# Moving the inverse DFT tables, splitting the last stage into pairs, and letting the first pairs skip a relayout: a fused attention and spectral-mixing kernel

## The chip, the cores and the metric

The kernel runs on one core of a Trainium2 chip. The metric is the device time of one execution in microseconds, as the median of several executions. All inputs start in the chip's main memory (HBM) and the output ends there. In the texts below PE is the matrix engine, DVE the vector engine, ACT the scalar engine, POOL the engine that here issues the weight, q and k transfers (with a cast to bf16 on the way), and SP the engine that issues the other transfers. PSUM is the memory of eight banks into which PE writes.

## The reference, cut to what matters

```python
def phi(x):                                    # q, k, v: 8 batches, 8 heads, 576 rows, 64 wide
    proj = einsum('bhsd,df->bhsf', x, w_phi)   # 64 -> 128 features
    proj = proj - max(abs(proj), axis=-1, keepdims=True)
    return concatenate([exp(proj), exp(-proj)], axis=-1)
num = phi(q) @ (phi(k)^T v);  den = phi(q) @ sum(phi(k)) + 1e-6
x = (num / den) reshaped to (8, 576, 512)      # heads side by side

X = rfft(x, axis=1)                            # along the 576 rows
Yr = Xr @ w_r[m] - Xi @ w_i[m]                 # for each of the first 64 modes m,
Yi = Xr @ w_i[m] + Xi @ w_r[m]                 # with a 512 x 512 matrix of its own
y = irfft(Y (other modes 0), n=576, axis=1)
u = x + y
out = u + maximum(u @ w_ch, 0)                 # w_ch: 512 x 512
```

The weights `w_r` and `w_i` are 64 x 512 x 512 in f32 each, 134 MB together. Everything else that is read is about 29 MB, and 9.4 MB are written.

## The kernel before, in words

**Order.** Two kinds of wrapper keep every instruction of an engine in the order in which the program text gives it (`InOrder`), so the text below is also the order of each engine's queue. That holds for the queues of POOL and SP too: an issue that has to wait for a free buffer holds up all issues behind it.

**Attention.** The work is cut into 16 units (`Unit`): four groups of two heads (g) times four pairs of batches (bp). A loop over n from -1 to 16 (lines 480 to 548) works on several units at once: P = unit n - 1 gets its forward Fourier transform (`freq`), Q = unit n its attention sums and quotients (`num`), K = unit n + 1 its features, R = unit n + 2 the turning of k. In the same stage the loads of later units are issued (`load_q`, `load_k`, `load_v`). q, k and v have two buffers each. `xs` holds the quotients of all units as bf16.

**Mixing.** A weight transfer (`wload`) brings eight modes of one of the two weights, for one group of 128 input channels, as 1 MB of bf16. There are 64 of them, each used by one `mix` of eight matmuls. They wait in the eight slots of pool `pw`, and the first ones also in five other places (`home`: memory of `yacc`, `XT` and `xs` that isn't needed yet). `next_w` issues the next transfer. `some(x)` does x mixes from the list `mixq` and, unless the mix used one of the five places, issues one transfer after each. A group's mixes come free when its fourth unit has had its `freq`, so the first mixes run in stage n = 4. X in the loop says how many mixes a stage does.

**Tables.** `CF` is the forward table. It is made from a table of sines `csf` at the start (`forward_table`, stage -1). The inverse tables `CI` and `CL` are made from the same `csf` in stage n = 0 (`inverse_table`): each of five blocks is scaled on DVE, transposed on PE in f32 and copied back by DVE.

**After the attention** (lines 549 to 672) 22 mixes are left. Between them items of a list `todo` are done (`fill`): first 37 items that turn each of the 36 chunks of x (128 rows by 512) and multiply it with `w_ch` into `xw` (`Channels`), then 36 calls of `absorb`, each of which adds the inverse transform of the first six octets of modes (48 modes) to one chunk of x and of xw. How many items go after a mix is n in that loop. The last eight mixes belong to octets 6 and 7. When an octet is complete, its sum `yst` and the product `zst` of that with `w_ch` are written by DMA into another layout (`put`): octets 0 to 5 into `yall` and `zall`, octets 6 and 7 into `yl`, two copies each, one copy issued by SP and one by ACT.

**The last stage** (lines 675 to 698) makes the 36 output chunks, in pairs and for each pair of batches one single chunk. For each chunk PE puts x and xw into two banks through the identity, adds the last two octets from `yl` with `CL`, ACT takes the ReLU of one (`rl`) and DVE adds the other (`of`). Four chunks fill an `of` tile of 1 MB, which SP stores; the single chunk (`ofr`) is stored as two pieces of 128 KB.

Of the kernel before, what the change touches and what calls it, by code (L numbers as in the profile page):

```python
# [10 lines left out]
F32 = mybir.dt.float32  # L11
BF16 = mybir.dt.bfloat16
# [8 lines left out]
NG = 4  # L21
# [22 lines left out]
def kernel(  # L44
# [260 lines left out]
    ident_f = const.tile([128, 128], F32, name="ident_f")  # L305
    make_identity(nc, ident_f)
    ident_b = const.tile([128, 128], BF16, name="ident_b")
    dve.tensor_copy(ident_b, ident_f)
# [3 lines left out]
    sp.dma_start(wpf[64:128, :], w_phi)  # L312
    si = const.tile([128, 5], I32, name="si")
# [5 lines left out]

    units = [Unit(g, bp) for g in range(NG) for bp in range(NP)]  # L320
    units[0].load_k()
    units[0].load_v()
    units[0].load_q()
# [9 lines left out]

    clear(XTb[0])
    wchb = const.tile([128, 4, 512], BF16, name="wchb")
    CF = const.tile([128, 6, 4, 64], BF16, name="CF")
    CI = const.tile([128, 5, 128], BF16, name="CI")
    CL = const.tile([128, 5, 128], BF16, name="CL")
# [35 lines left out]
    def inverse_table():  # L374

        cio = scr[:, 640:1280].rearrange("p (c m t r) -> p c m t r", c=5, t=2, r=2)
        for r in range(2):
            for t in range(2):
                dve.tensor_scalar_mul(
                    out=cio[:, :, :, t, r], in0=csf[:, :, r, 32 * t:32 * t + 32],  # L380
                    scalar1=(2.0 - 4.0 * r) / S_)
        for c in range(5):
            dve.tensor_scalar_mul(
                out=cio[:, c, 0, 0, :], in0=cio[:, c, 0, 0, :], scalar1=0.5)
            pct = one([128, 128])
            flat = cio[:, c].rearrange("p m t r -> p (m t r)")
            pe.transpose(pct, flat, ident_f)
            dve.tensor_copy(CI[:, c, :], pct)
            late = scr[:, 128 * c:128 * c + 128]
            dve.tensor_copy(  # L390
                late.rearrange("p (s m) -> p s m", s=4),
                flat[:, 96:128].unsqueeze(1).to_broadcast([128, 4, 32]))
            pct = one([128, 128])
            pe.transpose(pct, late, ident_f)
            dve.tensor_copy(CL[:, c, :], pct)


    def home(g, w):

        if g == 0 and w < 2:  # L400
            t = yacc.bitcast(BF16).rearrange("p o e -> p (o e)")[:, 4096 * w:4096 * w + 4096]
        elif g == 0 and w == 2:
            t = XTb[1].rearrange("p s b m -> p (s b m)")[:, 0:4096]
        elif g == 0 and w in (10, 11):
            t = xs[:, w - 8].rearrange("p b n d -> p (b n d)")[:, 0:4096]
        else:
            return pw.tile([128, MG, DMODEL], BF16, name="wt", tag="wt")
        return t.rearrange("p (m e) -> p m e", m=MG)

    def wload(g, w):  # L410
        wt = home(g, w)
        o, i = w // 2, w % 2
        pool.dma_start(
            wt, (moe_w_r, moe_w_i)[i][MG * o:MG * o + MG, g * 128:(g + 1) * 128, :].rearrange(
                "m p e -> p m e"))
        return wt

# [30 lines left out]
    wts = {}  # L448
    wq = [(g, mg) for g in range(2) for mg in range(2 * NO)]
    wq += [(g, mg) for g in (2, 3) for mg in range(12)]  # L450
    wq += [(g, 2 * o + i) for o in (6, 7) for g in (2, 3) for i in range(2)]
    order = list(wq)
    mixq = []

    def next_w(n):
        for _ in range(n):
            if wq:
                key = wq.pop(0)
                wts[key] = wload(*key)

# [15 lines left out]
    next_w(1)  # L476
    units[0].cast_k()
    units[0].turn_k()
    units[2].load_k()
    for n in range(-1, len(units) + 1):  # L480
# [16 lines left out]
        if P:  # L497
            P.freq()
            if P.bp == NP - 1:
                mixq += [key for key in order if key[0] == P.g and (P.g < 2 or key[1] < 12)]  # L500
        if K:
            K.cast_q()
# [39 lines left out]
        if n == 0:  # L542
            inverse_table()
# [10 lines left out]
    pst = ctx.enter_context(tc.tile_pool(name="pst", bufs=8, space=bass.MemoryType.PSUM))  # L554
# [7 lines left out]
    zall = pb.tile([96, B_, DMODEL], BF16, name="zall", bufs=1)  # L562
    yall = pw.tile([128, B_, DMODEL], BF16, name="yall", tag="wt")
    yl = pw.tile([128, B_, DMODEL], BF16, name="yl", tag="wt")


# [20 lines left out]
    def back(p, c, bp, table, src, r):  # L587

        if c < 8:
            pe.matmul(p, lhsT=table[r, c % 4, :], rhs=src[r, 2 * bp + c // 4, :],  # L590
                      start=(src is yall), stop=True)
        else:
            for i in range(2):
                pe.matmul(p[64 * i:64 * i + 64, :], lhsT=table[r, 4, 0:64],
                          rhs=src[r, 2 * bp + i, :], start=(src is yall), stop=True)

    def absorb(bp, n):

        r = slice(0, 96)
        x = chunk(bp, n)  # L600
        p = bank()
        back(p, n, bp, CI, yall, r)
        dve.tensor_tensor(out=x, in0=p.rearrange("p (g e) -> p g e", g=4), in1=x, op=ALU.add)
        q = bank()
        pe.matmul(q, lhsT=ident_b, rhs=xw[:, bp, n, :], start=True, stop=False)
        back(q, n, bp, CI, zall, r)
        act.copy(xw[:, bp, n, :], q)
# [14 lines left out]
    todo += [lambda c=c: absorb(*c) for c in chunks]  # L622
# [6 lines left out]
    def put(src, o, dst, copies):  # L629
        if o < 6:  # L630
            sp.dma_start(dst[16 * o:16 * o + 16], src)
        else:
            for e, s in zip((sp, act), copies):
                r = 32 * s + 16 * (o - 6)
                e.dma_start(yl[r:r + 16], src)

    steps = len(mixq)
    while mixq:
        key = mixq.pop(0)
        g, o, i = key[0], key[1] // 2, key[1] % 2  # L640
        if key not in wts:
            next_w(1)
        mix(*key, wts.pop(key), XTb[g % 2], bank)
        next_w(1)
        left = len(mixq)
        n = 5 if left < 8 else max(1, -(-(len(todo) - 36 - 3) // (left - 7)))
        if left == 0:
            n = len(todo)
        if g == NG - 1 and i == 1:
            py = pys.pop(o)  # L650
            yst = pb.tile([128, DMODEL], BF16, name="yst")
            dve.tensor_tensor(out=yst, in0=py, in1=yacc[:, o, :], op=ALU.add)
            put(yst, o, yall, (0, 2))
            fill(min(n, 1))
            pt = bank([128, 4, 128], BF16)
            for dc in range(4):
                pe.transpose(pt[:, dc, :], yst[:, dc * 128:(dc + 1) * 128], ident_b)
            yT = pb.tile([128, 4, 128], BF16, name="yT")
            act.copy(yT, pt)
            fill(min(n - 1, 1))  # L660
            pz = bank()
            for dc in range(4):
                pe.matmul(
                    pz, lhsT=yT[:, dc, :], rhs=wchb[:, dc, :],
                    start=(dc == 0), stop=(dc == 3))
            zst = pb.tile([128, DMODEL], BF16, name="zst")
            act.copy(zst, pz)
            put(zst, o, zall, (1, 3))
            fill(max(n - 2, 0))
        else:  # L670
            fill(n)
    assert not todo


    for bp in range(NP):
        of = [pw.tile([128, 4, DMODEL], F32, name="of", tag="wt") for _ in range(2)]
        ofr = pb.tile([128, DMODEL], F32, name="ofr")
        for ns in ((0, 1), (2, 3), (4, 5), (6, 7), (8,)):
            pq = [(bank(), bank()) for _ in ns]
            for n, (p, q) in zip(ns, pq):  # L680
                pe.matmul(p.rearrange("p (g e) -> p g e", g=4), lhsT=ident_b,
                          rhs=chunk(bp, n), start=True, stop=False)
                pe.matmul(q, lhsT=ident_b, rhs=xw[:, bp, n, :], start=True, stop=False)
            for a, (n, (p, q)) in enumerate(zip(ns, pq)):
                for b, t in enumerate((p, q)):
                    r = 64 * a + 32 * b
                    back(t, n, bp, CL, yl, slice(r, r + 32))
            for n, (p, q) in zip(ns, pq):
                rl = pb.tile([128, DMODEL], F32, name="rl")
                act.activation(rl, q, ACT.Relu)  # L690
                o = of[n // 4][:, n % 4, :] if n < 8 else ofr
                dve.tensor_tensor(out=o, in0=p, in1=rl, op=ALU.add)
            if ns[-1] in (3, 7):
                i = ns[-1] // 4
                sp.dma_start(
                    out[2 * bp + i, 0:512, :].rearrange("(p c) e -> p c e", c=4), of[i])
        for i in range(2):
            sp.dma_start(out[2 * bp + i, 512:576, :], ofr[64 * i:64 * i + 64, :])
# [31 lines left out]
```

## Time and profile before

| | us |
|---|---|
| median of 8 runs (lowest, highest) | 481.69 (480.99, 482.95) |
| the profiled execution | 481.51 |
| its span, first to last instruction | 479.7 |
| busy in the span: PE, DVE, ACT, POOL | 337.5, 312.3, 277.1, 103.9 |

The span leaves out 1.8 us of the profiled execution's own time. The mean clock granted to PE was 0.87 of full speed. A busy time is a sum over stages that have different limits, so it doesn't say what a change in one stage is worth.

How the profile is read: its page gives, over 40 equal slices of the span, the busy share of each engine in tenths, the share of the 16 DMA engines and the GB/s that they wrote. The table by stage gives the same for chosen stretches; there the DMA share counts overlapping packets and stands at about 1.25 when the transfers never pause. The chain of waits follows the work that ended last back from the end: start, length and what it was. The waits view sums for each engine what it waited for: total, number of waits, longest. All instructions have the line of a helper (L37), so they are told apart by the tiles that they write and read, `out<-in`.

### The profile page before, as it was taken

How to read it: one execution, taken by the hardware profiler on the slowest of the kernel's cores; microseconds unless marked ns; L12 is line 12 of the kernel's file. 1: busy time of each engine (PE TensorE's matmuls, PEld its weight loads, DVE VectorE, ACT ScalarE, POOL GpSimd, SP SyncE). 2: the span in 40 equal slices, each digit the busy share in tenths (PEclk: the TensorE clock that was granted, in tenths of full speed). 3: DMA queues.
4: the chain of work that ended last, by engine and by line, in shares of the span. 5: the costliest groups of instructions: out<-in, count | busy, mean ns of one | idle time of the engine just before them, and what ended most of it. 6: DMA issues, size and time to landing. Idle time of an engine off the chain costs nothing.

```text
span 479.7 us, 8392 instructions
## 1 busy us (share of the span) xinstructions
PE 337.5 (70%) x3227; PEld 204.2 (43%) x3254; DVE 312.3 (65%) x568; ACT 277.1 (58%) x471; POOL 103.9 (22%) x139
## 2 busy tenths in 40 slices
PE   2552777876677787776857738559976577888894
PEld 1341455654555454554645426434433233333221
DVE  5677397796797788788787776752322113765695
ACT  3761477668679678658648628512433224565684
POOL 8332032112152142123032122041111111000000
PEclk9985567688998888889779777887999989999999
DMA  8999999998999999999999999999999999995398
GB/s 136 212 213 209 214 201 216 210 205 131 206 209 217 217 200 217 215 203 217 218 201 215 218 206 207 207 207 207 207 213 214 214 212 216 207 223 101 131 368 312
DMA packets 111896, 100.23 MB, mean 209 GB/s; under 512 B 17008, under 2 KB 110320, under 8 KB 110832
## 3 DMA queue, kind: packets, MB, share of 16 engines
q0 software_dynamic: 84496, 76.03, 97.6%
q1 hardware_dynamic: 26784, 23.14, 18.6%
q10 hardware_dynamic: 576, 0.52, 0.5%
q8 instruction: 25, 0.41, 0.3%
q14 instruction: 15, 0.12, 0.1%
HBM read 163.64 MB, written 9.44 MB: 361 GB/s over the span
## 4 chain that ended last, share of the span: by engine, by line
DMA 63%; DVE 10%; PE 9%; issue 9%; ACT 4%; POOL 2%; SPq 1%; DVEq 0%; POOLq 0%; ACTq 0%
DMA wt<-in_moe_w_i_dram 28%; DMA wt<-in_moe_w_r_dram 20%; DMA qb<-in_q_dram 8%; DMA kb<-in_k_dram 5%; PE pt L37 5%; PE one L37 4%; DVE mk L37 2%; POOL wt L37 2%; DVE va L37 2%; DVE nd L37 2%; DMA kf<-in_k_dram 2%; SPq L37 1%; DVE mq L37 1%; PE two L37 1%; ACT AB L37 1%
## 5 line engine op out<-in xcount | busy, mean ns | idle before, releaser
L37 ACT ACTIVATE AB<-two 128x1024 bf16<-128x1024 f32 x64 | 62.0, 1021 | 44.4 <-DVE mk L37 44.1
L37 ACT CAST xw<-pt 128x512 bf16<-128x512 f32 x72 | 41.9, 586 | 71.5 <-PE pt L37 66.4
L37 ACT ACTIVATE AQ<-two 128x1024 bf16<-128x1024 f32 x64 | 62.7, 1043 | 23.6 <-PE two L37 16.6
L37 DVE TENSOR_TENSOR nd<-one,e 128x390 f32<-128x390 f32 x48 | 26.9, 560 | 48.8 <-PE one L37 48.8
L37 POOL DMA_DIRECT2D wt<-in_moe_w_r_dram x29 | 25.6, 882 | 100.8 <-PE pt L37 35.1
L37 PE MATMUL one<-kvz,AQ 128*128 128x65 bf16 x512 | 30.1, 204 | 19.7 <-ACT kvz L37 14.5
L37 PE MATMUL one<-va,AB 128*128 128x65 bf16 x512 | 30.0, 219 | 18.9 <-DVE va L37 18.8
L37 DVE TENSOR_TENSOR va<-vn,ee 128x1152 bf16<-128x1152 f32 x32 | 42.0, 1357 | 0.0
L37 DVE COPY xT<-pt 128x512 bf16<-128x512 bf16 x36 | 15.2, 423 | 41.1 <-PE pt L37 41.1
L37 DVE TENSOR_REDUCE mk<-two 128x8 f32<-128x1024 f32 x32 | 39.0, 1220 | 4.0 <-PE two L37 4.0
L37 POOL DMA_DIRECT2D wt<-in_moe_w_i_dram x30 | 26.5, 882 | 67.6 <-PE pt L37 33.2
L37 PE MATMUL pt<-wchb,xT 128*128 128x512 bf16 x136 | 39.6, 410 | 0.8 <-DVE xT L37 0.5
L37 PEld LDWEIGHTS <-XT 128*32 128x32 bf16 x512 | 21.6, 165 | 42.6 <-issue 35.2
L37 PEld LDWEIGHTS <-xs 128*128 128x128 bf16 x304 | 29.2, 112 | 22.6 <-issue 11.8
L37 DVE TENSOR_REDUCE mq<-two 128x8 f32<-128x1024 f32 x32 | 37.7, 1217 | 1.1 <-PE two L37 1.1
L37 PEld LDWEIGHTS <-AQ 128*128 128x128 bf16 x512 | 25.3, 104 | 30.5 <-issue 27.3
L37 POOL DMA_DIRECT2D qb<-in_q_dram x32 | 22.9, 720 | 60.2 <-DVE nd L37 33.0
L37 PEld LDWEIGHTS <-AB 128*128 128x128 bf16 x512 | 25.3, 115 | 24.8 <-issue 12.9
L37 POOL DMA_DIRECT2D kb<-in_k_dram x32 | 22.9, 717 | 58.3 <-PE one L37 19.7
L37 DVE TENSOR_TENSOR xs<-pt,xs 128x512 bf16<-128x512 f32 x36 | 24.2, 691 | 13.5 <-PE pt L37 13.0
L37 PE MATMUL pt<-wt,XT 128*32 128x512 bf16 x176 | 15.6, 427 | 24.4 <-DMA wt<-in_moe_w_i_dram 14.6
L37 PE MATMUL one<-ident_b,kb 128*128 128x128 bf16 x144 | 15.8, 260 | 23.2 <-DMA kb<-in_k_dram 20.7
(94 smaller groups left out, 667.1 us busy)
## 6 DMA issues: line engine op xcount, KB each, us to landing
wt<-in_moe_w_i_dram POOLq DMA_DIRECT2D x30, 1024.0 KB, 27.0
wt<-in_moe_w_r_dram POOLq DMA_DIRECT2D x29, 1024.0 KB, 25.9
vn<-in_v_dram SPq DMA_DIRECT2D x32, 256.0 KB, 7.8
out_dram<-of SPq DMA_DIRECT2D x8, 1024.0 KB, 4.3
kb<-in_k_dram POOLq DMA_DIRECT2D x32, 128.0 KB, 20.5
qb<-in_q_dram POOLq DMA_DIRECT2D x32, 128.0 KB, 17.1
kf<-in_k_dram SPq DMA_DIRECT2D x32, 32.0 KB, 6.2
vn<-in_v_dram SPq DMA_DIRECT2D x32, 32.0 KB, 6.5
```

Source lines behind the costliest of these rows:

```text
L37: ins = f(*args, **kwargs)
```

## The change

- `inverse_table` is gone, and with it its f32 transposes. After the attention, `inverse_tables` computes `CI`, `CL` and a third table `CM` straight from integers, rows being modes: three iotas on POOL, bit fields of the row number and small scalars on DVE, then for each table a product, a reduction to one period, a sine on ACT and a scaling. It is the first item of `todo`.
- At the start the loads of unit 0's k and the first weight transfer go ahead of the identity and the iotas on POOL; q goes ahead of v; unit 0's k is turned before the forward table is computed.
- In stage n = 4 two mixes more are done, right after `freq`. One `next_w(1)` ahead of the loop moves to the start.
- `absorb` becomes a class `Absorb` of three steps; its last three chunks are spread over the end of the last mix. The number of items after each mix is counted anew.
- Both copies into `yl` are issued by SP.
- The last stage becomes a class `Last`: PSUM is split into two pools (four single banks for q, two double banks for p); the q side and ReLU of a pair are done one pair ahead of its p side; DVE adds two chunks in one instruction; each pair is stored by itself (512 KB).
- The first two pairs read only octet 6 from `yl` and take octet 7 straight from `yst` and `zst` with `CM`.

```diff
+    units[0].load_k()
+    next_w(1)
+    ident_f = scr[:, 2176:2304]
+    make_identity(nc, ident_f)
...
+    units[0].load_q()
+    units[0].load_v()
     si = const.tile([128, 5], I32, name="si")
     pool.iota(si[:, 0:4], [[1, 4]], base=0, channel_multiplier=4)
...
-    units[0].load_k()
-    units[0].load_v()
-    units[0].load_q()
...
+    units[0].cast_k()
+    units[0].turn_k()
     clear(XTb[0])
...
-    next_w(1)
-    units[0].cast_k()
-    units[0].turn_k()
     units[2].load_k()
...
                 mixq += [key for key in order if key[0] == P.g and (P.g < 2 or key[1] < 12)]
+            if n == 4:
+                some(2)
...
-        if n == 0:
-            inverse_table()
...
+    def inverse_tables():
+        flat = zall.rearrange("p b e -> p (b e)").bitcast(F32)
+        tok, ang, rnd = (flat[:, 640 * i:640 * i + 640] for i in range(3))
...
+        pool.iota(toki[:, 0:512], [[1, 4], [4, 128]], base=0, channel_multiplier=0)
+        pool.iota(toki[:, 512:640], [[0, 2], [1, 64]], base=512, channel_multiplier=0)
+        pool.iota(pi, [[0, 1]], base=0, channel_multiplier=1)
+        dve.tensor_copy(tok, toki)
...
+        def bits(src, shift, mask):
...
+            dve.tensor_scalar(out=t, in0=src, scalar1=shift, scalar2=mask,
+                              op0=ALU.logical_shift_right, op1=ALU.bitwise_and)
+            dve.tensor_copy(f, t)
...
+        for dst, m, r, only in ((CI, mode, r, None), (CL, late, r, None), (CM, last, rm, b0)):
+            n = 512 if only is not None else 640
...
+            dve.tensor_scalar(out=ang[:, :n], in0=tok[:, :n], scalar1=m, scalar2=ph,
+                              op0=ALU.mult, op1=ALU.add)
+            dve.tensor_scalar(out=rnd[:, :n], in0=ang[:, :n], scalar1=1.0 / S_, scalar2=MAGIC,
+                              op0=ALU.mult, op1=ALU.add)
+            dve.tensor_scalar(out=rnd[:, :n], in0=rnd[:, :n], scalar1=-MAGIC,
+                              scalar2=-float(S_), op0=ALU.add, op1=ALU.mult)
+            dve.tensor_tensor(out=ang[:, :n], in0=ang[:, :n], in1=rnd[:, :n], op=ALU.add)
+            act.activation(rnd[:, :n], ang[:, :n], ACT.Sin, scale=2.0 * math.pi / S_)
+            dve.tensor_scalar_mul(out=dst.rearrange("p c s -> p (c s)"), in0=rnd[:, :n],
+                                  scalar1=amp)
...
-            for e, s in zip((sp, act), copies):
+            for s in copies:
                 r = 32 * s + 16 * (o - 6)
-                e.dma_start(yl[r:r + 16], src)
+                sp.dma_start(yl[r:r + 16], src)
...
+    todo = [inverse_tables] + todo
...
-        n = 5 if left < 8 else max(1, -(-(len(todo) - 36 - 3) // (left - 7)))
-        if left == 0:
-            n = len(todo)
+        n = -(-max(len(todo) - 33, 0) // (left - 7)) if left > 7 else -(-len(todo) // max(left, 1))
...
+            if end:
+                ab[-3].sums()
+                ab[-3].keep_x()
...
             act.copy(yT, pt)
+            if end:
+                ab[-2].sums()
+                ab[-2].keep_x()
+                ab[-3].keep_w()
...
             put(zst, o, zall, (1, 3))
+            if end:
+                ab[-2].keep_w()
+                ab[-1].all()
...
+        def straight(self, which):
+            if self.early:
+                for a, n in enumerate(self.ns):
+                    pe.matmul((self.q if which else self.p)[a], lhsT=CM[:, n],
+                              rhs=(yst, zst)[which], start=False, stop=True)
...
+    seq = [Last(bp, ns) for bp in range(NP) for ns in ((0, 1), (2, 3), (4, 5), (6, 7), (8,))]
+    seq[0].base(1)
+    seq[0].late(1)
+    seq[0].straight(1)
+    seq[0].relu()
+    for g, s in enumerate(seq):
+        t = seq[g + 1] if g + 1 < len(seq) else None
+        if t:
+            t.base(1)
+        s.base(0)
+        if t:
+            t.late(1)
+        s.late(0)
+        s.straight(0)
+        if t:
+            t.straight(1)
+            t.relu()
+        s.store()
```

`base` puts x (0) or xw (1) of a pair into its banks, `late` adds the part from `yl`, `relu` is two ACT instructions into one tile, and `store` is the DVE add over both chunks and the issue of the store.

## The prediction

> **What bounds the kernel now.** I read the page first: its slices by time, then its bytes.
>
> ```profile
> DMA  8999999998999999999999999999999999995398
> GB/s 136 212 213 209 214 201 216 210 205 131 206 209 217 217 200 217 215 203 217 218 201 215 218 206 207 207 207 207 207 213 214 214 212 216 207 223 101 131 368 312
> ...
> HBM read 163.64 MB, written 9.44 MB: 361 GB/s over the span
> ```
>
> The span is 479.7 us and a slice 12. The DMA digit is 9 nearly everywhere up to slice 35, while no compute engine is full throughout: up to 439 us the kernel is a stream of loads. Three places fall out: slice 0, slice 9 (108 to 120 us) and slices 36 and 37 (432 to 456 us). Elsewhere a faster engine buys nothing. The table by stage sharpens the first two; its last two columns are the DMA share (1.25 when full) and GB/s.
>
> ```profile
> 0.00:3.00 3.00, 0.00 (x0) 0.00 (x0) 0.47 (x3) 1.28 (x1) 2.26 (x12) 1.00 0.08 21
> 3.00:6.00 3.00, 0.56 (x4) 0.34 (x4) 2.35 (x8) 0.00 (x0) 3.00 (x5) 1.00 0.91 114
> 6.00:9.00 3.00, 0.65 (x5) 0.34 (x4) 2.86 (x5) 0.00 (x0) 3.00 (x5) 1.00 1.05 185
> ...
> 111.00:114.00 3.00, 2.19 (x21) 1.20 (x24) 2.69 (x6) 2.83 (x6) 1.43 (x2) 0.70 0.80 159
> 114.00:117.00 3.00, 2.89 (x40) 1.79 (x33) 1.70 (x4) 2.98 (x6) 0.00 (x0) 0.73 0.69 96
> 117.00:120.00 3.00, 1.72 (x23) 1.48 (x20) 2.80 (x7) 1.36 (x5) 2.05 (x3) 1.00 0.42 40
> 120.00:123.00 3.00, 2.69 (x37) 1.92 (x35) 3.00 (x5) 2.02 (x5) 1.26 (x3) 1.00 1.16 195
> ```
>
> Start: 3 x (1.17 + 0.34 + 0.20) / 1.25 = 4.1 us of full transfer are missing. Hole: 3 x (0.45 + 0.56 + 0.83 + 0.09) / 1.25 = 4.6 us. In the hole all 13 weight homes are full and the first that comes free is reissued at 117.16 (timeline of POOL). The rest is the tail, from the chain of waits:
>
> ```profile
> 402.04 36.89 DMA wt<-in_moe_w_i_dram
> 438.97 0.70 PE pt L37 x7
> 439.69 0.69 DVE yst L37
> 440.38 0.61 DVE xs L37
> 441.01 0.58 ACT xw L37
> 441.60 0.50 ACT yT L37
> ...
> 443.21 0.59 ACT zst L37
> 443.83 4.03 DMA yl<-zst
> ```
>
> The last weight is used at 438.97; 8.9 us later (447.9) `yl` is complete and the 36 output chunks begin. From 450 us DVE adds without a pause, 0.69 us each, 1.41 us a pair; the last ends at 474.58, and 5.1 us later its store is in. So time = end of stream (439.0) + 40.7 + 1.8 outside the span: 481.51 us for the profiled execution, 0.18 under the runs' median of 481.69, well inside their spread; I make the sum against 481.51. About 0.2% (1 us) is what can be told from no change.
>
> **A rule that speaks against any gain in the stream.** In 288 to 348 us (slices 24 to 28), weights alone, 207 GB/s arrive as bf16, which is 414 GB/s of f32 read. The Trainium skill, "DMA: Bandwidth & Descriptors", section "Specifications", gives about 358 GB/s of HBM for a core. By that, 173.1 MB need 483 us, the kernel is already at its limit (361), the holes are an illusion, and only the tail could gain: about 479. The trace runs at 414 for 60 us on end, so holes can be filled; I count them.
>
> **Start.** POOL issues the first `kb` at 1.96, behind a memset, the affine select and four iotas (1.2 us from 0.74). These now stand behind it, and the first 1 MB weight goes third in POOL's queue, at about 2.3 instead of 6.34. Then the share is nil to 2.3, 0.9 to 3.8, full afterwards: (2.3 x 1.25 + 1.5 x 0.35) / 1.25 = 2.7 us missing instead of 4.1, **1.4 us gained** (0.5 to 2). Moved past: `ident_b` waits for POOL until 3.7 instead of 1.34, so DVE's casts, `clear` and table run about 2 us later, to about 11.3; the first `mk` reduction stands at 11.52 anyway, and the stage is held at 15.61 by `kf` of unit 1, whose place on SP (11th and 12th issue) is unchanged. On SP q's two go before v's four; v is first read at 21.3. If this cover went, compute would start up to 2 us later, which is not the stream. Weight issues before the first mix stay 13.
>
> **Hole.** Adds of `nd` that open a stage start at 29.85, 59.90, 76.78, 93.66, 110.54: one gap of 30.05 among 16.88. The long one holds the inverse tables (DVE 43.16 to 54.2, ten f32 transposes with a DVE copy each). Moving them takes 13.2 us out of the compute chain. Not all survives: the `kb` issued at 67.74 needs 20 to 26 us in a full queue and is turned at 100.03, so some 7 of the 13 stay. In stage n = 4 two mixes now go right after `freq`, so the first reissue moves ahead of `num(6)`, about 2 us, and five weights are asked for in that stage instead of three. 117.2 - 7 - 2 = 108, before the hole opens at 111. Price: the two mixes (1.96 us on PE at 112.69) stand before `num(0)`, and DVE waits that long; compute is ahead there, so nothing. In n = 7 two mixes fewer: the running total of reissues is never behind. **4.3 us of 4.6** (0 if the lead doesn't reach n = 4).
>
> **The tables' new place.** First item after the first tail mix. POOL: three iotas; by 128x4 0.13 and 128x64 0.27 us (2.4 ns a column) 1.3 + 0.4 + 0.1 = 1.8 us in front of the next weight issues, hidden by 40 us of queued loads (the chain's 321.52 40.41). DVE: nine bit fields of two and 17 scalars, 35 instructions at 0.17 (`mk` 128x18 0.17, 128x2 0.16), 6.0 us; one 640-wide cast 0.7; twice 4 x 0.66 + 0.83 + Sin 0.74 on ACT + 0.2 for two hand-overs = 4.4, the 512-wide one 3.6: 19.1 us. The table load (1.28 in the page's start) waits beside DVE; a second one for Relu isn't seen and would lie in the wait for `yl`. PE turns two chunks and then waits for `xT`, a DVE copy behind all this: mix 324.3, weight issue to 326.5, iotas to 328.3, DVE to 347.4, `xT` 347.9, where it was 326.5: **a stall of 21.4 us**. Does it reach the end? Loads go on, since seven or eight are asked for ahead and only four would lie unread. PE catches up in the time it now waits for weights:
>
> ```profile
> PE pt L37 <- DMA wt<-in_moe_w_i_dram: 14.6, 9, 4.1
> ...
> PE pt L37 <- DMA wt<-in_moe_w_r_dram: 9.8, 7, 3.3
> ```
>
> 24.4 us, less the 3.3 before the stall: 21.1. One more `Absorb` (0.65) falls before the last mix. Left over 21.4 + 0.65 - 21.1: **0.9 us lost** (0 to 4).
>
> **Tail.** With T the start of the last mix. `keep_w` goes behind `yT`: `zst` ends at T + 4.25 instead of 4.82. Both copies go by SP, the second 0.6 us after the first, where ACT sent it at once: `yl` complete at T + 8.9 as now. Meanwhile pair 0 (and pair 1's `q`) is done from `yst` and `zst`; pair 1's `p` stands on PE behind pair 2's `late(1)`, which waits for `yl`: p at 8.9 + 0.4 + 0.43, its add at T + 9.8. Then 14 pairs and 4 singles. PE's pitch is 1.30 a pair where nothing held it (448.22 to 449.52) and 0.87 a single; ACT 2 x 0.60; DVE one 1024-wide add, 1.22 by the reductions of that width. PE is now last: 14 x 1.30 + 4 x 0.87 = 21.7, last add ends at T + 32.2, against 35.6: 3.4; end of store as before. Bounds: at DVE's 1.24 1 us more, at the old 1.41 1.5 less; the hand-over of PSUM from one pool to two may cost some tenths. **3.2 us gained**.
>
> **Stores, and a rule against them.** 1 MB stores become 512 KB. Rows 455 to 475 show 352 to 375 GB/s at share 0.92 to 0.97, so about 385 when full: 8.9 MB in 23.1 us from T + 12, in by T + 37, just inside compute's T + 37.3. The same page, section "Bandwidth", asks for DMAs of 1 MiB or more for over 75% of peak (64 KB gets 32%). Taken at two thirds of 435, 290 GB/s, the stores would end at T + 44 and the tail lose 3.6. But those are DMAs by themselves; here 128 KB stores land in 3.9 us and 1 MB ones in 4.3, with the next already issued, so the fixed part overlaps. I take the trace.
>
> Sum: 481.5 - 1.4 - 4.3 + 0.9 - 3.2 = **473.5 us**.
>
> **Rivals.**
> *Only part of it comes* (0.22): compute is held by loads, not by the tables, and the hole stays half, or PE ends 3 us late. For: the 6 us of slack of `kb`. Against: in 16 to 130 us PE waits for no load. 475.5 to 479.
> *The stores become the bound* (0.06): as by the rule, 480.3; for it, the share is already 0.95.
> *Slower* (0.10): the table block isn't absorbed. Everything behind 20.5 us of stall adds to the end, and 8.9 us of gains are eaten at a stall of 29.4. That is so when the 35 narrow instructions, each on the result before, cost 0.40 instead of 0.17; at 0.45 the stall is 31.2, PE 10.7 late, and the time 483.3. For: no chain of such ops is in the trace. Against: 128x18 and 128x2 rows.
>
> **Numbers.** Forecast case 0.52 (471 to 475.5), better 0.07 (a pitch of 1.24 and no lag), partial 0.22, stores 0.06, no change 0.03, slower 0.10. Range 469.5 to 479, holding 0.8: faster 0.87, same 0.03, slower 0.10.
>
> **What would show it.** Right: share near 1.25 throughout 4 to 120 us; last mix at about 434; `nd` adds 17 us apart from the start; a gap of about 20 us on PE soon after the first tail mix, mixes late against their loads, and caught up by about 425; adds of 1.22 us 1.30 apart; span near 471.7. Wrong: a dip in DMA left at 105 to 120; PE still waiting for nothing but itself before the last mix; store share at 1 with DVE idle behind it.

## The result, and the profile after

The changed kernel takes 477.42 us (median of 11 runs, 476.15 to 479.41) where the kernel before, run beside it, takes 481.74: a ratio of 0.9915 with an interval of 0.9899 to 0.9931, or about 4.1 us less. The forecast was 8.2 us less. The profiled execution shown below took 479.41 us, with a span of 477.3; it is the slowest of the eleven, 2 us above their median, so its own end is read with that in mind.

The page after, its slices (11.9 us each) and its bytes:

```profile
DMA  8999999999999999999999999999999999994498
GB/s 121 223 205 207 215 214 205 214 217 197 214 203 215 216 211 208 215 210 210 217 210 208 220 204 207 207 208 207 207 207 211 217 214 221 207 207 78 163 342 317
...
HBM read 163.64 MB, written 9.44 MB: 363 GB/s over the span
```

Slice 9, which had 131 GB/s, has 197: the hole is closed. Slice 0 has less than before, 121 instead of 136. The mean over the span, 363 GB/s, and the 365 of the best version below are above the 358 that the rule quoted in the forecast allows a core; the holes could be filled. The table by stage (the last two columns are DMA share and GB/s) tells the same more finely:

```profile
0.00:3.00 3.00, 0.00 (x0) 0.00 (x0) 0.00 (x0) 1.28 (x1) 1.96 (x7) 1.00 0.11 15
3.00:6.00 3.00, 0.90 (x8) 0.64 (x8) 0.84 (x4) 0.58 (x1) 2.86 (x8) 1.00 1.13 129
6.00:9.00 3.00, 1.45 (x8) 0.58 (x6) 1.45 (x4) 0.99 (x2) 2.93 (x6) 1.00 1.00 140
111.00:114.00 3.00, 0.17 (x4) 0.17 (x7) 2.73 (x6) 2.64 (x5) 1.60 (x2) 1.00 1.43 191
114.00:117.00 3.00, 2.94 (x43) 2.38 (x39) 2.57 (x7) 2.26 (x8) 1.82 (x3) 1.00 1.30 193
117.00:120.00 3.00, 2.67 (x33) 1.88 (x34) 3.00 (x5) 2.02 (x5) 2.69 (x4) 1.00 1.23 208
120.00:123.00 3.00, 2.02 (x42) 1.55 (x39) 2.83 (x6) 1.35 (x2) 0.42 (x1) 1.00 1.22 201
```

From 111 to 120 us the share stands at 1.23 to 1.43, where it was 0.42 to 0.80. At the start it rises no faster: the forecast's own sum of missing share, over these three rows and 9 to 12 us (1.20), gives 3.7 us against 4.1, not 2.7. The last weight lands at 435.4 us instead of 438.9, so the stream gave 3.5 us.

The timeline of PE shows the new stalls of the weight phase (start, duration, operation, and in brackets the idle time before it with what ended it):

```profile
342.29 1.49 PE L37 MATMUL pt<-wchb,xT 128*128 128x512 bf16 x3 [19.26 <-DVE xT L37]
...
403.29 0.59 PE L37 MATMUL pt<-yall,CI 96*128 96x512 bf16 x1 [2.86 <-issue]
...
406.61 0.59 PE L37 MATMUL pt<-zall,CI 96*128 96x512 bf16 x1 [2.31 <-issue]
406.99 0.63 PE L37 MATMUL pt<-yall,CI 96*128 96x512 bf16 x1
```

The first is the forecast stall behind the tables: 19.3 us against 21.4. The mixes, 17.9 us behind their loads after it, are 3.3 us behind at 399.7. The other two were not forecast: the first `Absorb` needs the sums of octet 5, which are on their way into `yall` (issued at 397.19, landed at 403.20) and `zall` (400.51, 406.52). After them the matmuls take 0.63 us; where PE isn't held up so long they take 0.38. So in this execution PE reaches the last mix at 437.89, 2.5 us after its weight.

The tail, from the chain of waits:

```profile
441.63 0.58 ACT zst L37
442.22 0.99 ACT xw L37 x2
443.25 1.88 PE qq L37 x8
445.13 0.43 PE pp L37 x2
```

`zst` ends 4.33 us after the last mix (T), as forecast; the next PE work waits until ACT has emptied the last bank for `xw`, at T + 5.4. PE's line for it, and then DVE's timeline, which continues it:

```profile
443.25 0.59 PE L37 MATMUL qq<-xw,ident_b 128*128 128x512 bf16 x2 [0.70 <-ACT xw L37]
```

```profile
446.52 1.23 DVE L37 TENSOR_TENSOR of<-pp,rl 128x1024 f32<-128x1024 f32 x1 [3.90 <-PE pp L37]
448.68 3.85 DVE L37 TENSOR_TENSOR of<-pp,rl 128x1024 f32<-128x1024 f32 x3 [0.93 <-ACT rl L37]
452.70 0.69 DVE L37 TENSOR_TENSOR ofr<-pp,rl 128x512 f32<-128x512 f32 x1 [0.18 <-PE pp L37]
454.06 2.54 DVE L37 TENSOR_TENSOR of<-pp,rl 128x1024 f32<-128x1024 f32 x2 [0.67 <-PE pp L37]
```

The first add starts at T + 8.6 and the last ends at T + 35.3; before, the last ended at T + 35.6. The adds of pairs do come 1.3 us apart, but the DVE waits around each single (0.18 before it, 0.67 behind it) return four times: 6.70 us per pair of batches, more than the 6.46 of before and the 6.07 forecast. What the tail gains is at its end: 4.1 us from the last add to the end of the span instead of 5.1. The page's rows of DMA issues (count, size, median us to landing), of before and then after:

```profile
out_dram<-of SPq DMA_DIRECT2D x8, 1024.0 KB, 4.3
```

```profile
out_dram<-of SPq DMA_DIRECT2D x16, 512.0 KB, 2.9
```

### The profile page after: what moved, and what is told of

Same layout as the page of the kernel before. It is cut to its first block, busy times and chain, and to the rows that moved or that the text cites. A ratio compares the mean times of both kernels' runs of the same rounds, so it can differ in the third digit from the quotient of the medians.

```text
span 477.3 us, 8430 instructions
## 1 busy us (share of the span) xinstructions
PE 334.6 (70%) x3225; PEld 201.3 (42%) x3252; DVE 318.4 (67%) x579; ACT 280.6 (59%) x476; POOL 104.9 (22%) x142
## 4 chain that ended last, share of the span: by engine, by line
DMA 45%; PE 28%; DVE 13%; issue 7%; ACT 4%; POOL 1%; DVEq 0%; SPq 0%; POOLq 0%; ACTq 0%
DMA kb<-in_k_dram 25%; PE pt L37 19%; DMA wt<-in_moe_w_r_dram 10%; DMA wt<-in_moe_w_i_dram 5%; PE qq L37 4%; DVE mk L37 3%; DMA qb<-in_q_dram 3%; PE one L37 3%; DVE nd L37 2%; PE pp L37 2%; DVE va L37 2%; ACT AB L37 2%; DVE mq L37 2%; DVE zall L37 2%; DMA vn<-in_v_dram 2%
## 5 line engine op out<-in xcount | busy, mean ns | idle before, releaser
L37 PE MATMUL pt<-wchb,xT 128*128 128x512 bf16 x136 | 38.0, 394 | 19.6 <-DVE xT L37 19.3
L37 PE MATMUL one<-va,AB 128*128 128x65 bf16 x512 | 31.0, 223 | 23.8 <-DVE va L37 23.6
L37 POOL DMA_DIRECT2D wt<-in_moe_w_r_dram x29 | 25.6, 883 | 86.5 <-PE one L37 32.9
L37 PEld LDWEIGHTS <-xs 128*128 128x128 bf16 x304 | 30.3, 115 | 23.8 <-issue 11.8
L37 ACT COPY kT<-one 128x512 bf16<-128x512 bf16 (+1 forms) x32 | 19.7, 662 | 22.4 <-PE one L37 22.0
L37 PE MATMUL one<-ident_b,kb 128*128 128x128 bf16 x144 | 14.6, 245 | 24.9 <-DMA kb<-in_k_dram 18.2
L37 PEld LDWEIGHTS <-XT 128*32 128x32 bf16 x512 | 20.1, 172 | 27.6 <-issue 21.7
```

The source lines that it names most:

```text
L37: ins = f(*args, **kwargs)
```

## The experiments

Times are medians; ratios are to runs of the kernel before on the same chip. T is the start of the last mix in the profile of the kernel spoken of.

**1. Three items kept back more** (on the changed kernel):

```diff
-        n = -(-max(len(todo) - 33, 0) // (left - 7)) if left > 7 else ...
+        n = -(-max(len(todo) - 36, 0) // (left - 7)) if left > 7 else ...
```

> The changed kernel with one number altered: 36 items of the list are kept for the last eight mixes instead of 33, so three channel items stand again between the last sum of octet 5 and the first chunk that reads it. Theory 'PE late': the last mix starts 2.5 us after its weights landed because PE, still late from the tables, runs into the first chunk before the transfers of octet 5 are in (two waits of 2.9 and 2.3 us around 400 to 407 us). Then these waits shrink to under 1 us, the last mix starts within 1 us of the landing of its weights, and the time falls by about 2 us to 475.5. Rival 'only the tables count': PE does the same work later, the last mix is late by the same 2.5 us, time 477.4 +- 0.5.

476.89 us (476.55 to 477.30), 0.9894 [0.9874, 0.9914]. One wait is left of 1.65 us, the matmuls behind it stay at 0.38, and the last mix starts 0.2 us after its weight:

```profile
401.35 0.38 PE L37 MATMUL pt<-zall,CI 96*128 96x512 bf16 x1 [1.65 <-issue]
```

So without the long waits for octet 5 the 2.5 us are gone. The waits alone do not make them: both are in the profiles of experiments 2, 3, 6 and 7 too (1.9 to 3.6 us each), and there the last mix starts 0.0 to 0.5 us after its weight. The 2.5 us are of the one profiled execution. Over the runs the gain is about 0.5 us by the medians, with intervals that overlap; the spread is 0.8 us over six runs, where it was 3.3 over eleven.

**2. No tables behind the attention.** The three tables are filled with zeros, so the inverse transform is left out of the output.

```diff
-    todo = [inverse_tables] + todo
+    todo = [blank_tables] + todo      # three memsets
```

> The changed kernel with the computation of the three inverse tables left out (they are filled with zeros in the same place). Theory 'PE late': without the 17 us on DVE PE is never late against its weights in the stage behind the attention, the last mix starts when its weights land, so the time falls by the 2.5 us of lateness, to about 475. Rival 'absorbed': the tables are hidden entirely and the lateness comes from the order of the last items alone; then the time stays at 477.4 +- 0.5.

478.14 us (477.57 to 479.93), 0.9925 [0.9904, 0.9946]. The stall of 19 us is gone and nothing is gained: by the runs, the tables in their new place are free. The profile shows a detail that the time hides. PE is early enough to wait for the last weight, 2.4 us sooner than in the profile of the changed kernel, although both waits for octet 5 are there:

```profile
435.49 0.67 PE L37 MATMUL pt<-wt,XT 128*32 128x512 bf16 x8 [1.62 <-DMA wt<-in_moe_w_i_dram]
```

The last add ends at T + 35.4, as it did, but the last stores are slow in this execution: issued from 470.3 us on, they land 4.1 to 4.6 us later, where the changed kernel's take 2.5 to 2.7. So the end comes only 0.7 us sooner. What stands beside them is told in the last section.

**3. No pair takes the short cut.**

```diff
-            self.early = bp == 0 and ns[0] < 4
+            self.early = False
```

> The changed kernel with the early pairs turned off: all pairs read both octets from yl. Theory 'no gain from the short cut': in the profile of the changed kernel the first add starts 0.24 us after yl is complete (446.52 against 446.28), so the short cut bought almost nothing: without it the first add starts some 1.2 us later, but the second and third follow without the extra matmuls (0.86 us a pair): time 0 to +0.7 us against the changed kernel. Rival 'it hides the relayout': all of the wait of 3.3 us comes back, +3 us.

480.51 us (479.48 to 481.39), 0.9970 [0.9956, 0.9984], 3.1 us slower than the changed kernel. T is 435.4 here; `yl` is complete at 443.75, and DVE's timeline shows what follows:

```profile
446.95 1.23 DVE L37 TENSOR_TENSOR of<-pp,rl 128x1024 f32<-128x1024 f32 x1 [6.86 <-PE pp L37]
449.30 1.23 DVE L37 TENSOR_TENSOR of<-pp,rl 128x1024 f32<-128x1024 f32 x1 [1.12 <-PE pp L37]
451.07 1.23 DVE L37 TENSOR_TENSOR of<-pp,rl 128x1024 f32<-128x1024 f32 x1 [0.55 <-PE pp L37]
```

The first add starts at T + 11.6 instead of T + 8.6: the steps through PE and ACT that precede a first add then lie behind `yl` and not beside its transfer. Without the short cut the new last stage would gain nothing: its span ends at T + 43.0, where that of the kernel before ends at T + 40.7.

**4. The tables alone, taken out of the kernel before** (zeros, as in 2).

```diff
         if n == 0:
-            inverse_table()
+            dve.memset(CI, 0.0)
+            dve.memset(CL, 0.0)
```

> The kernel before with the computation of the two inverse tables left out (filled with zeros in stage n = 0). Theory 'the tables alone made the hole': compute reaches the first mixes some 13 us sooner, less what loads hold back, the dip in the DMA share at 111 to 120 us goes, and the time falls by 4 to 4.6 us to about 477.3, although the start and the stage n = 4 are as before. Rival 'the two early mixes close it': the dip stays at half, the time falls by 2 us or less.

478.00 us (476.62 to 479.00), 0.9914 [0.9892, 0.9935]. Its table by stage:

```profile
111.00:114.00 3.00, 2.31 (x41) 1.92 (x41) 2.97 (x6) 1.88 (x5) 2.33 (x4) 1.00 1.46 192
114.00:117.00 3.00, 1.85 (x26) 1.02 (x19) 3.00 (x5) 2.74 (x4) 1.95 (x3) 1.00 1.24 185
117.00:120.00 3.00, 3.00 (x46) 2.29 (x43) 2.78 (x6) 0.15 (x1) 0.00 (x0) 1.00 1.26 204
```

Taking away the tables closes the hole by itself, and gives 3.9 us, with no other edit. That is all that the stream gains in the changed kernel, so the reordered start adds nothing to it.

**5. The reordered start alone, in the kernel before.**

```diff
+    units[0].load_k()
+    next_w(1)
...
+    units[0].load_q()
+    units[0].load_v()
...
-    units[0].load_k()
-    units[0].load_v()
-    units[0].load_q()
...
+    units[0].cast_k()
+    units[0].turn_k()
     clear(XTb[0])
...
-    next_w(1)
-    units[0].cast_k()
-    units[0].turn_k()
```

> The kernel before with the reordered start alone (k and the first weight ahead of the iotas, q ahead of v, k turned before the forward table). The forecast's step: 1.4 us more of the stream at the start, so about 480.3. My theory now: the first 1 MB weight stands in POOL's queue in front of unit 0's q, which then lands at about 17 us instead of 10; stage 0 begins 4 us later, the compute chain that fixes the first reissue of a weight (117.2 us in the kernel before) is later by up to that, and the hole at 108 to 120 us grows: +2 to +4 us, 484 to 485.5.

484.84 us (484.06 to 486.47), 1.0056 [1.0038, 1.0074]: 2.9 us slower, where the forecast's step has 1.4 gained. The hole is deeper:

```profile
114.00:117.00 3.00, 1.98 (x29) 1.47 (x32) 2.33 (x6) 3.00 (x6) 1.14 (x2) 0.91 0.17 47
...
120.00:123.00 3.00, 2.53 (x35) 1.91 (x28) 2.76 (x7) 1.42 (x4) 1.06 (x2) 1.00 0.07 3
```

The stage-opening `nd` adds are at 33.7 and 63.9 instead of 29.9 and 59.9, the first reissue at 121.1 instead of 117.2. The size was as I expected; the cause that I had given for it fell in experiment 9.

**6. The first weight behind unit 0's q, in the changed kernel** (`next_w(1)` moved from `units[0].load_k()` to behind `units[0].load_q()`).

> The changed kernel with the first weight issued behind unit 0's q instead of ahead of it. Theory: stage 0 begins 3 to 4 us earlier and the last weight lands at about 434.0, as where only the tables were left out of the kernel before, instead of 435.3: 1 to 1.5 us faster than the changed kernel, 476. Rival: the hole is closed with room to spare, so the compute chain's lead buys nothing: 477.4, within 0.5.

478.34 us (476.18 to 479.22), 0.9915 [0.9880, 0.9949]: the rival was right, no difference can be seen. But stage 0 opens only 1.0 us earlier (32.8 us), since `kf` of unit 1 lands as late as before (18.1): this does not undo the loss of experiment 5. Experiment 13 does.

**7. No extra mixes in stage n = 4** (the two lines `if n == 4: some(2)` taken out of the changed kernel).

> The changed kernel without the two extra mixes in stage n = 4. Theory: moving the tables alone closes the hole, as it did in the kernel before, so 477.4 within 0.5, and the share stays at 1.2 or above from 105 to 120 us. Rival (the forecast's step): two mixes less in n = 4 make the first reissue 2 us later and three weights are asked for instead of five: a dip between 108 and 120 us and up to 2 us slower, 479.

477.51 us (476.80 to 478.03), 0.9897 [0.9868, 0.9927]: nothing lost. The first reissue is at 112.4 with them and at 112.3 without. Stage n = 4 then opens earlier, as DVE's timeline shows, the changed kernel first, then this one:

```profile
108.00 0.56 DVE L37 TENSOR_TENSOR nd<-one,e 128x390 f32<-128x390 f32 x1 [6.28 <-PE one L37]
```

```profile
104.28 0.57 DVE L37 TENSOR_TENSOR nd<-one,e 128x390 f32<-128x390 f32 x1 [2.61 <-PE one L37]
```

**8. The singles joined.** On the kernel of experiment 1, the four single chunks (64 rows used of each) become two pairs, put at the end:

```diff
-    seq = [Last(bp, ns) for bp in range(NP) for ns in ((0, 1), (2, 3), (4, 5), (6, 7), (8,))]
+    seq = [Last([(bp, n), (bp, n + 1)]) for bp in range(NP) for n in (0, 2, 4, 6)]
+    seq += [Last([(bp, 8), (bp + 1, 8)]) for bp in (0, 2)]
```

> The changed kernel with the absorbs' reserve of three items more, and with the four single chunks (64 rows) joined two by two and put at the end, so no pair of 128-row chunks shares PE with a single of 64 rows. Theory: the stages that hold both shapes lose about 0.63 us for each of the four singles; 14 to 17 stages of 1.30 us and no mixed ones: last add 1.4 to 2 us earlier after the last mix, 475 to 475.5 against 476.9 with the reserve alone. Rival: the stores are the bound in the tail (512 KB each at a share near 1), and the last one ends when it did: 476.9 within 0.4.

476.56 us (475.94 to 477.65), 0.9880 [0.9850, 0.9910]: 0.3 less than experiment 1, within the spread. The profile shows that both theories are half right. PE's timeline, the stage with a single in the changed kernel first (`450.48`, tiles 32*64 and 32*128), then the same place here:

```profile
449.38 0.39 PE L37 MATMUL qq<-yl,CL 32*128 32x512 bf16 x2
449.39 0.39 PE L37 MATMUL pp<-yl,CL 32*128 32x512 bf16 x2
...
450.48 0.40 PE L37 MATMUL qq<-yl,CL 32*64 32x512 bf16 x2
450.81 0.39 PE L37 MATMUL pp<-yl,CL 32*128 32x512 bf16 x2
```

```profile
454.72 0.39 PE L37 MATMUL qq<-yl,CL 32*128 32x512 bf16 x2
454.73 0.39 PE L37 MATMUL pp<-yl,CL 32*128 32x512 bf16 x2
```

Four matmuls of one shape start together; two of each shape start 0.33 us apart. With one shape at a time the last add ends at T + 32.9 instead of T + 35.3: 2.4 us. But the last store lands at T + 37.8, only 0.6 us sooner than in experiment 1, because the stores are now the bound: 512 KB take 8 packets of 4 KB (0.161 us each) on each of 16 DMA engines, 1.29 us, just the 1.30 of a pair, and from the fourth store on they land 3.2 to 4.5 us after issue instead of 2.7.

**9. Where the loss of the start comes from.** The kernel of experiment 5, with the first weight behind unit 0's q:

> The kernel before with the reordered start, but the first weight issued behind unit 0's q. Theory: the 2.9 us that the reordered start alone costs come from q waiting behind 1 MB of weight; with q first they are gone, 481.5 within 0.7. The forecast's step (no harm, the transfers begin earlier): 480.5. Rival: the harm is in k's turn ahead of the forward table, or in q ahead of v: 484.8 as with the weight first.

484.62 us (482.90 to 486.05), 1.0061 [1.0044, 1.0078]: q lands at 7 to 8 us and the loss stays, so my cause was wrong. What stage 0 waits for is `kf` of unit 1. The same line of DVE's timeline in the kernel before, and here:

```profile
15.61 0.23 DVE L37 CAST kb<-kf 128x128 bf16<-128x128 f32 x1 [1.61 <-DMA kf<-in_k_dram]
```

```profile
18.52 0.23 DVE L37 CAST kb<-kf 128x128 bf16<-128x128 f32 x1 [5.27 <-DMA kf<-in_k_dram]
```

Its two 32 KB pieces are issued by SP at 7.2 and 8.4 us (7.3 and 8.1 before), but land at 17.8 and 18.4 instead of 14.5 and 15.5.

**10. The first weight where it was, behind unit 1's k,** all else of the new start kept:

```diff
     units[0].load_k()
-    next_w(1)
...
     units[1].load_k()
+    next_w(1)
     units[1].load_v()
```

> The kernel before with the reordered start, but the first weight issued behind the k of unit 1, where it stood before. Theory: the 2.9 us came from unit 1's k landing 3 us later (the pieces kf at 18.4 us instead of 15.5) behind a weight in transfer, and stage 0 with it: with the weight back, the first add of stage 0 starts at 30 us again instead of 33, and the time is 482 within 0.7. Rival: it is k's turn ahead of the forward table or q ahead of v, the time stays at 484.7 and the first add at 33.

481.95 us (480.44 to 483.41), 1.0003 [0.9989, 1.0017], the first `nd` add at 30.13:

```profile
15.43 0.23 DVE L37 CAST kb<-kf 128x128 bf16<-128x128 f32 x1 [2.17 <-DMA kf<-in_k_dram]
```

This settles it: the 2.9 us come from the place of the early weight alone. Its issue is at 2.8 us in experiment 5 and at 4.7 in experiment 9, 2.5 us or more ahead of `kf`; here it is at 6.9 (6.3 in the kernel before), 1 us ahead or less. The other edits of the start (iotas, q ahead of v, k turned first) show no effect here. The Trainium skill, "DMA: Bandwidth & Descriptors", section "Queues, rings and completion order", says that a DMA engine takes turns between the queues that have work for it, packet by packet; SP's small pieces then pay for a large transfer on POOL's queue. 7.2 us to landing growing to 10.6 agrees with that; no run separates this from other reasons for sharing.

**11. The joined singles in fifth and sixth place,** so that the last store is one issue:

> The kernel with the joined singles again, these two now in fifth and sixth place instead of at the end, so the last store is one issue of 512 KB and not four of 256 KB at 0.7 us each. Theory: PE, DVE and the stores all stand at 1.30 us a pair; the last store is in about 37.1 us after the last mix instead of 37.8: 0.5 to 0.7 us faster than with the singles at the end, about 476.0. Rival: the backlog of the stores alone sets the end, whatever the order: 476.6 within 0.4.

476.42 us (474.86 to 476.86), 0.9879 [0.9853, 0.9905]. The last store again lands at T + 37.8, now 4.6 us after its issue; the rival was right. Where the joined singles are stored, from 453 to 457 us, the DMA engines are as busy as elsewhere (share 0.99 and 0.93), but only 250 and 300 GB/s are written instead of about 400, and stores land 4.8 us after issue behind it instead of 3.7. The rows of the singles are written in pieces of 2 KB (in every version), those of the 512 KB stores in pieces of 4 KB.

**12. Five stores left out in the middle** of the kernel of experiment 8 (those rows of the output are not written):

> The kernel with the singles joined at the end, with five of the sixteen 512 KB stores in the middle left out (all of the second pair of batches and one of the third; those rows of the output are not written). Theory: behind the fourth store the queue of stores runs 1.3 to 1.7 us late and, as 512 KB take as long as a pair on PE, never catches up; with five stores fewer it is drained, a store lands 2.7 us after its issue again and the end comes 1 to 1.3 us earlier, about 475.4. Rival: the stores' lateness isn't in the end, which is set by the last add and four issues: 476.6 within 0.4.

475.01 us (474.45 to 477.39), 0.9868 [0.9840, 0.9897]. By the time alone the theory looks right, by the profile it isn't: T is 434.7 there, 2.1 us earlier than in experiment 8, and the last store lands at T + 37.8 once more, with the last adds at the same T + 32.9. The stores left out did drain the queue: the three behind them land in 2.6 to 2.7 us. The next one, issued at 460.93, takes 3.5, and at the end stand the four stores of 256 KB, which are slow while the engines are busy:

```profile
468.00:470.00 2.00, 0.00 (x0) 0.00 (x0) 0.00 (x0) 0.00 (x0) 0.00 (x0) 1.00 0.98 231
470.00:472.00 2.00, 0.00 (x0) 0.00 (x0) 0.00 (x0) 0.00 (x0) 0.00 (x0) 0.59 0.82 269
```

So the end is set here for the most part by the 1 MB that goes out in pieces of 2 KB, and less by the backlog. What a drained queue would give behind one last store of 512 KB stays open.

**13. The best put together:** experiment 11 with the weight behind unit 1's k.

> The changed kernel with the reserve of three items more, the singles joined in the middle, and the first weight behind unit 1's k. Theory: stage 0 opens 3 to 4 us earlier, but in the changed kernel the first weight comes free in time anyway, so 476.4 within 0.5 as with the weight first. Rival: the earlier compute is a lead that the stream can use: 475.5.

475.95 us (475.24 to 476.63), 0.9879 [0.9861, 0.9896], 6.1 us under the kernel before by the medians. Stage 0 opens at 30.2 again, the last weight lands at 434.7. It is the fastest complete version here, though not beyond the spread of experiments 8 and 11. Experiment 11 differs from it by the early weight alone and is 0.5 us slower by the medians: in the changed kernel a loss by the early weight, if there is one, is within the spread.

## Why the prediction was half right

**Hole: right, for part of its reasons.** 4.3 us were forecast, 3.9 measured with the tables alone taken out. That about 7 us of lead would remain at n = 4 was right: stage 4 opens at 103.7 instead of 110.5 in experiment 4, and at 104.3 in experiment 7. The two extra mixes, counted for 2 us more, gain nothing: standing before `num(0)`, they take 3.7 us of that lead (108.0), which the forecast put at nothing, and the first reissue is at 112.4 with them or without, where 108 was forecast. The hole closes all the same.

**Start: the step that failed first.** The forecast took 1.4 us gained from the DMA share and said that `kf` of unit 1 has its place on SP unchanged, so the stage is held at 15.61. Its place was unchanged, its landing was not: with a 1 MB weight issued 2.5 us ahead of it, it lands 3 us later (experiment 9). Alone that is 2.9 us of time. The sum also took the transfers as full from 3.8 us on; at 6 to 9 us the share is 1.00 and 140 GB/s arrive, where 185 did. In the changed kernel no loss shows beyond the spread (experiment 13 against 11): with the tables gone from stage 0 the hole stays closed all the same. But no gain shows either: 0 for 1.4.

**Tables: right in mechanism and size.** 19.3 us of stall against 21.4, and it is caught up: experiment 2 gains nothing by leaving them out. The lateness of 0.9 forecast for it is there in size (0.5 by the medians of experiment 1), but it takes two things together: the rest of the stall (3.3 us at 399.7) and a wait that the sum lacked, of the first `Absorb` for octet 5's transfers. In the profiles the waits without the tables leave PE on time (experiment 2), and so do the tables without the long waits (experiment 1); with both, the last mix is 0.0 to 2.5 us late. "PE ends late" was rival 1; the sum had only half of its cause.

**Tail: the largest miss.** 3.2 us forecast, 1.3 measured (the span ends at T + 39.4 instead of T + 40.7). The mis-sized term is the last add, put at T + 32.2 and found at T + 35.3. Of these 3.1, 1.0 is the start: the second add begins at T + 10.8, not T + 9.8. The forecast had it wait for `yl`, which is complete at T + 8.4; what it waits for is PE, which is held 0.7 us at the hand-over of PSUM (until 443.25; it was given "some tenths") and then has 5.3 us of work for the first pairs without a pause. The other 2.1 is the pitch: 0.87 was taken for a single, as if it ran beside a pair at no cost. On PE the two stages that mix a single with a pair take 1.4 us each (from 449.71 to 451.13 and to 452.54), where 0.87 and 1.30 were counted. The Trainium skill, "TensorEngine Tiling (Array Packing)", section "Key Properties", says that a change of tiling mode drains the array; the 0.33 us between the two shapes agree, and joining the singles takes 2.4 us off. Against that, 1.0 came back that had been counted at nothing: the last piece of 128 KB, behind stores of 512 KB and no longer of 1 MB, lands 2.5 us after its issue instead of 3.6.

**Stores.** That they fit "just inside" compute held while the mixed stages gave them pauses. Without these they set the end (experiments 8 and 11). The rule of 1 MB per DMA did not bite: 402 to 409 GB/s were written with 512 KB each (experiment 8, 456 to 468 us).

Together: 3.5 (stream, from the profile) - 0.5 (lateness, by the medians) + 1.3 (tail, from the profile) = 4.3, against 4.1 measured, and 8.0 in the forecast's sum from the profiled execution. Missing are 1.4 of the start, 0.8 of the hole and 1.9 of the tail, less 0.4 of lateness that didn't come.

## What to carry to other kernels

Ask of every transfer that is moved forward which small transfers are in flight with it, on any queue, and what waits for those; an unchanged place in the queue is not an unchanged landing. Count a stage by what its matmuls' shapes allow side by side, not by their mean duration. And when a change has several parts, cost what the next bound is worth: here PE, DVE and the stores all stand near 1.3 us a pair (1.30, 1.23 and 1.29), so freeing one of them gives a fraction.

## What the runs showed of the hardware beyond expectation

Loads of instructions appear among the data transfers. In the tail of experiment 8 the view of DMA queues for 452 to 455 us has one:

```profile
q8 instruction: 1, 0.02, 2.9%
```

That is one packet of 16 KB, which in the trace holds one DMA engine for 1.41 us from 452.42. The store issued at 451.35 lands 3.0 us after the one before it, where 1.3 is the rule. Such a packet is in the tail of every kernel run here (0.9 to 1.7 us each). Where stores come at the rate that they are written, the delay stays to the end; where singles leave pauses, the next stores land in 2.7 us again. One or two packets of 8 KB (0.3 to 1.0 us each) also come in each tail. In experiment 12 one stands at 462.28 us, beside the first store that is slow again behind the drained queue; in experiment 2 at 469.16, ahead of the slow last stores. In the profile of the changed kernel one (468.40, 0.31 us) is followed by no such delay. That these packets are the cause of the later landings is argued from the order in time, not tested.

Half the clock can follow a short stall. Behind 2.9 and 2.3 us of waiting, PE ran at a granted clock of 0.50 from 404 to 412 us, its chunk matmuls came 0.43 us apart where they come 0.22 apart from 413 us on, and the mixes' lateness grew from 3.3 to 10.1 us. With one wait of 1.65 us the clock stayed at 1.00 (experiment 1). The length of the wait alone doesn't decide it: in the kernel before, a wait of 3.1 us for a weight ends at 373.08, and the clock stays at 1.00 before and behind it (369 to 377 us).
